# Attention results kept channels by tokens and normalised through DRAM, in a fused attention and GLU kernel

## The chip, the cores and the metric

One core of one Trainium2 chip. The metric is the device time of one launch, in microseconds. Before the change it is 891.36 us, the median of three runs (887.86, 891.71, 891.36).

## What is computed

One transformer block on 2048 tokens of 512 channels in float32, with 32 heads of 16 channels. The tokens are cut into four segments of 512. Within a segment there is causal softmax attention; across segments there is a running memory (M, z) that each segment reads before it adds to it:

```python
for s in range(N):
    p = softmax(qs @ ks.T * scale + mask)
    a_dot = p @ vs
    a_mem = (phi(qs) @ M) / (phi(qs) @ z + 1e-6)
    outs.append(g * a_mem + (1 - g) * a_dot)
    M, z = M + phi(ks).T @ vs, z + sum(phi(ks))
x = x + ga * (concat(outs) @ wo)
x = x + gb * ((h(x) @ w_gate) * (h(x) @ w_up)) @ w_down
```

Both halves begin with a layer norm that is scaled and shifted from c and w_mod.

## The kernel before

**Units and turns.** Attention is done in 32 units. Unit u is four heads of one segment (segment u//8, group of eight heads g = u//2 % 4, half u % 2). A main loop (from L998) runs turns v = -2 to 32, each of five slots. In turn v the scores of units v+1 and v+2 are formed once to find their row maxima (`q_step`: TensorE, then reductions on VectorE), the scores of unit v are formed again, transposed and with the maxima subtracted, and exponentiated (`k_step`: TensorE, then the 128x1024 `pt` on ScalarE, then the causal select on GpSimd), and in slot 1 the products with v of unit v-1 are summed (`av_step`: 32 matmuls `tb`, then the copy `tsb` on ScalarE). `tb` has 17 useful rows for each head, 16 channels and the sum of the exponentials.

The maxima (`nm`) are split into `nh`, transposed on TensorE (`ntp`), copied to `nt`, and two DMAs on the sync engine's queue (SP) put them into `qst`, where `k_step` of the next turn reads them (`n_split`, `n_step`). k and q of a head group go through DRAM as well (`kd`, `qd`), and `load` brings them back as `kst` and `qst`, three turns ahead.

**The result of a unit.** `t_step`, in slot 4 of turn v, transposes `tsb` of unit v-1 with four TensorE transposes into `tr` (tokens by channels), takes the reciprocal of the sums and multiplies, both on VectorE, into `orow`. After the second half of a head group GpSimd adds the memory term `memb`, which had been written to `memd` by `a_mem` and read back, and a DMA stores `orow` in `od`, tokens by channels. When the output projection comes, `wo_load` reads `od` back (`orl`), `wo_op` transposes it to channels by tokens with four transposes for each head group (`op`), and splits it into a high part `oH` (ScalarE) and a rest `oL` (VectorE). `wo_mm` multiplies both by wo (`wops`).

**Fill.** Everything else that TensorE has to do (projections `kps`, `qps`, `vps`, memory, output projection, second layer norm) comes from two generators, `fill_a` and `fill_b`, which give pieces of work into four of the five slots. Each piece costs credit, and a turn brings 5.5 of it, which is 24 matmuls of 512 columns; a piece that yields False ends its slot at once, and unused credit is kept for later turns. `fill_b` starts when `fill_a` is done: it opens new pools, loads wo and `orl`, and runs `wo_op` and `wo_mm` of segments 0, 1 and 2. Segment 3 comes after the loop, and then the GLU.

TensorE runs in the order of the program, and so does VectorE from the loop on. The order on ScalarE, GpSimd and SP is set by the scheduler, but each of them takes its instructions strictly in turn: what waits holds up what stands behind.

Below, "interval u" is the time from the copy `tsb` of unit u-1 to that of unit u.

Of the kernel before, what the change touches and what calls it, by code (L numbers as in the profile page):

```python
# [58 lines left out]
def tile_kernel(ctx, tc, x, wq, wk_, wv, wo, beta, w_gate, w_up, w_down, c, w_mod, out):  # L59
# [76 lines left out]
    od = [dram.tile([4, P, D], F32, name=f"od{s}") for s in range(NSEG)]  # L136
# [64 lines left out]
    def ln(pool, hpool, xt, s, sc, sh, pfx, hb, fast, kept_h=None):  # L201
# [5 lines left out]
        for d in range(KT):  # L207
            h = pool.tile([P, L], F32, tag="hf" if kept_h is None else "orl", name=f"{pfx}hf{s}_{d}", bufs=hb[2])
# [45 lines left out]
    orows, mems, ptiles, sels, tbs, tsbs = {}, {}, {}, {}, {}, {}  # L254
# [76 lines left out]
    def av_step(u, kb):  # L331
# [19 lines left out]
        if kb == 2:  # L351
            tsbs[u] = ap.tile([P, L], F32, tag="tsb", name=f"tsb{u}", bufs=2)
            act.activation(tsbs[u], tbs.pop(u), AF.Copy)  # L353

    def t_step(u):

        s, g, jq = u // 8, u // 2 % 4, u % 2
        ug = u // 2
        h0 = jq * HQ
        if jq == 0:  # L360
            orows[ug] = wpool.tile([P, 4, HG, DH], F32, tag="orow", name=f"orow{ug}", bufs=2)
            if s > 0:
                mems[ug] = ap.tile([P, 4, HG, DH], F32, tag="memb", name=f"memb{ug}", bufs=2)
                nc.sync.dma_start(mems[ug].rearrange("p t h e -> p (t h e)"), memd[s][g])
        orow = orows[ug]
        tsb = tsbs.pop(u)
        tr = pst([P, 4, 4, 32], "sm", f"tr{u}", F32)
# [6 lines left out]
        if jq == 0:  # L374
            return
        if s > 0:
            nc.gpsimd.tensor_add(orow, orow, mems.pop(ug))
        if ug < NSEG * NG - 1:
            nc.sync.dma_start(od[s].rearrange("t p c -> p t c")[:, :, g * P:(g + 1) * P],
                              orow.rearrange("p t h e -> p t (h e)"))  # L380
# [35 lines left out]
    def wo_load(s, pool):  # L416
        rw = []
        for t in range(4):
            a = pool.tile([P, D], F32, tag="orl", name=f"orl{s}_{t}", bufs=4)
            n = D - P if s == NSEG - 1 else D  # L420
            pin(nc.sync.dma_start(a[:, 0:n], od[s][t][:, 0:n]))
            rw.append(a)
        return rw

    def wo_op(s, pb, rw, us, gs=range(NG)):

        for g in gs:
            op = bank(f"op{s}_{g}")
            for t in range(4):
                a = rw[t][:, g * P:(g + 1) * P]  # L430
                if s == NSEG - 1 and g == NG - 1:
                    a = orows[NSEG * NG - 1][:, t].rearrange("p h e -> p (h e)")
                TP(op[:, t * P:(t + 1) * P], a, ident)
            oH = pb.tile([P, L], F32R, tag="oH", name=f"oH{s}_{g}", bufs=6)
            oL = pb.tile([P, L], F32R, tag="oL", name=f"oL{s}_{g}", bufs=6)
            act.activation(oH, op, AF.Copy)
            us.append((oH, oL))
            yield 0.45
            pin(vec.tensor_sub(oL, op, oH.bitcast(F32)))
            if g % 2 == 1:  # L440
                yield False
# [175 lines left out]
    stage = [("ph", 3), ("ph", 3), ("ph", 3), ("mem", 1), ("pkr", 1), ("f", 2)] + [("x", 4)] * 6  # L617
# [135 lines left out]
    memq, nkq = [], {}  # L753

    def mem_step():
        while memq:
            w = next(memq[0], None)
            if w is not None:
                return w
            memq.pop(0)  # L760
# [616 lines left out]
```

## Time and profile before

| | |
|---|---|
| median of three runs | 891.36 us |
| the profiled execution, its own time | 892.53 us |
| its span | 890.8 us |
| mean granted TensorE clock | 0.987 |
| TensorE matmuls busy | 848.3 us (95%) |
| VectorE busy | 660.8 us (74%) |
| ScalarE busy | 471.0 us (53%) |
| GpSimd busy | 417.9 us (47%) |
| moved by DMA | 124.85 MB, mean 140 GB/s |

The attention loop fills the span from about 60 us to 523 us, then comes a passage of some 60 us into the GLU, and the GLU runs to the end. In the rows of a timeline the first number is the start in us, the second the time until the last instruction of a merged row ended, and a bracket gives the idle time of the engine ahead of it and what ended it. Matmuls are pipelined, so what a matmul costs TensorE is read from the distance of two starts. "128x512 f32" is partitions by elements. In a row of windows the columns are the window's length, then busy time (and number of instructions) of TensorE, its weight loads, VectorE, ScalarE and GpSimd, then the granted clock, the busy share of the DMA engines, and GB/s.

### The profile page before, as it was taken

The numbers are of one execution on the slowest core, as the hardware profiler recorded it, in microseconds if no ns is written. First come the engines' busy times: TensorE is split into PE (matmuls) and PEld (weight loads), VectorE is DVE, ScalarE is ACT, GpSimd is POOL, SyncE is SP. The second block draws the span as 40 slices with busy tenths as digits, with TensorE's granted clock in tenths as the row PEclk, the third lists the DMA queues.
The fourth block names the chain that finished last, engine by engine and source line by source line (L and its number), as shares of the span: only waits on it lengthen the run. The fifth ranks groups of instructions, "written<-read, shape, count | busy, mean of one in ns | idle before, by whom it ended". The sixth has DMA issues, their size and how long they took to land.

```text
span 890.8 us, 14534 instructions
## 1 busy us (share of the span) xinstructions
PE 848.3 (95%) x4951; PEld 598.1 (67%) x4952; DVE 660.8 (74%) x1756; ACT 471.0 (53%) x730; POOL 417.9 (47%) x564
## 2 busy tenths in 40 slices
PE   8988999999999999999899898999999999999998
PEld 5755666665665556565556466878878888887886
DVE  8588877897788987678788649798884856666532
ACT  3756867777677775577444654333262622333321
POOL 4544545566546574466623423887500746560000
PEclk9998999999999999999899999999999999999999
DMA  7673543746446543657861453444402341222032
GB/s 237 216 229 114 185 122 104 240 155 199 139 125 201 163 140 123 184 164 225 257 214 61 131 164 105 144 143 123 167 26 97 93 140 48 71 54 92 0 116 95
DMA packets 103515, 124.85 MB, mean 140 GB/s; under 512 B 11984, under 2 KB 71376, under 8 KB 103440
## 3 DMA queue, kind: packets, MB, share of 16 engines
q1 hardware_dynamic: 103296, 123.90, 45.3%
q8 instruction: 39, 0.64, 0.3%
q14 instruction: 36, 0.29, 0.1%
q10 hardware_dynamic: 144, 0.02, 0.0%
HBM read 80.17 MB, written 43.45 MB: 139 GB/s over the span
## 4 chain that ended last, share of the span: by engine, by line
PE 65%; DVE 16%; DMA 8%; ACT 5%; POOL 3%; issue 2%; SPq 1%; DVEq 0%; POOLq 0%; ACTq 0%
PE g L86 20%; PE acc L86 14%; PE tb L86 6%; DVE q L40 6%; PE k L86 5%; PE q L86 5%; PE vps L86 4%; PE kps L86 2%; PE qps L86 2%; PE wops L86 2%; ACT pt L324 2%; DMA qd<-q 2%; DMA qst<-qd 1%; PE up L86 1%; DVE nm L40 1%
## 5 line engine op out<-in xcount | busy, mean ns | idle before, releaser
L40 DVE CUSTOM_DVE_ANT_0 q<-q,cmask 128x384 f32<-128x384 f32 (+3 forms) x512 | 246.7, 508 | 57.9 <-PE q L86 47.8
L324 ACT ACTIVATE pt<-k 128x1024 f32<-128x1024 f32 x160 | 163.8, 1024 | 76.5 <-PE k L86 74.2
L327 POOL TENSOR_SCALAR_AFFINE_SELECT pt<-pt 128x256 f32<-128x256 f32 (+1 forms) x224 | 99.0, 455 | 175.4 <-ACT pt L324 172.0
L86 PE MATMUL q<-kst,qst 96*128 96x384 bf16 (+3 forms) x512 | 102.4, 303 | 9.2 <-DVE nm L40 6.5
L86 PE MATMUL k<-qst,kst 98*128 98x384 bf16 (+3 forms) x512 | 98.4, 305 | 8.0 <-ACT pt L324 6.3
L400 POOL TENSOR_TENSOR w<-w 128x256 f32<-128x256 f32 (+1 forms) x84 | 72.4, 872 | 60.4 <-DMA w<-in_w_up_dram 57.8
L397 POOL TENSOR_TENSOR AL<-w,AH 128x512 fp32r<-128x512 f32 (+1 forms) x42 | 59.3, 1412 | 55.4 <-ACT AH L396 54.4
L86 PE MATMUL tb<-pt,v 128*32 128x512 f32 (+3 forms) x1024 | 76.3, 438 | 0.9 <-POOL pt L327 0.9
L86 PEld LDWEIGHTS <-kst 98*128 98x128 bf16 x512 | 39.0, 99 | 50.9 <-issue 42.8
L40 DVE DVE_READ_ACCUMULATOR2_ANT nm<- 128x1 f32 x512 | 72.0, 141 | 0.0
L396 ACT ACTIVATE AH<-w 128x512 fp32r<-128x512 f32 (+2 forms) x88 | 47.3, 565 | 45.7 <-POOL w L400 22.4
L86 PEld LDWEIGHTS <-qst 96*128 96x128 bf16 x512 | 43.8, 98 | 36.2 <-issue 10.0
L1319 DVE TENSOR_TENSOR mL<-mid,mH 128x512 fp32r<-128x512 f32 (+1 forms) x44 | 32.2, 735 | 41.5 <-ACT mH L1318 40.5
L86 PE MATMUL acc<-DH,mH 128*128 128x512 f32 x144 | 57.2, 397 | 0.0
L86 PE MATMUL acc<-DH,mL 128*128 128x512 f32 x144 | 56.6, 393 | 0.2 <-DVE mL L1319 0.2
L86 PE MATMUL acc<-DL,mH 128*128 128x512 f32 x144 | 56.5, 393 | 0.0
L86 PEld LDWEIGHTS tb<-pt,v 128*32 128x32 f32 x1024 | 28.7, 110 | 40.4 <-issue 34.7
L1318 ACT ACTIVATE mH<-mid 128x512 fp32r<-128x512 f32 (+1 forms) x44 | 27.1, 626 | 51.2 <-PE acc L86 50.2
L1114 ACT ACTIVATE p<-g 128x512 f32<-128x512 f32 (+1 forms) x22 | 13.1, 597 | 69.2 <-PE g L86 69.2
L397 DVE TENSOR_TENSOR AL<-w,AH 128x512 fp32r<-128x512 f32 (+3 forms) x44 | 33.8, 772 | 18.5 <-ACT AH L396 18.5
L353 ACT ACTIVATE tsb<-tb 128x512 f32<-128x512 f32 x32 | 19.1, 596 | 38.7 <-PE tb L86 38.6
L86 PE MATMUL g<-t_0H,AH 128*128 128x512 f32 (+1 forms) x88 | 34.6, 394 | 1.1 <-DVE u L1123 1.0
(278 smaller groups left out, 2097.9 us busy)
## 6 DMA issues: line engine op xcount, KB each, us to landing
kst<-kd SPq DMA_DIRECT2D x32, 384.0 KB, 4.3
qst<-qd SPq DMA_DIRECT2D x32, 384.0 KB, 5.1
wm<-in_w_mod_dram SPq DMA_DIRECT2D x24, 256.0 KB, 5.2
kd<-k SPq DMA_DIRECT2D x16, 384.0 KB, 3.8
qd<-q SPq DMA_DIRECT2D x16, 384.0 KB, 3.2
w<-in_w_gate_dram SPq DMA_DIRECT2D x40, 128.0 KB, 2.5
w<-in_w_up_dram SPq DMA_DIRECT2D x40, 128.0 KB, 3.1
wd<-dwd SPq DMA_DIRECT2D x6, 768.0 KB, 4.6
```

What stands on the lines that cost most here:

```text
L40: i = getattr(self.eng, name)(*a, **k)
L86: return pe(nc.tensor.matmul(*a, **k))
L324: lpt[0] = act.activation(pt, kp, AF.Exp, scale=0.25)
L327: sels[u, i] = nc.gpsimd.affine_select(w, w, pattern=[[0, w.shape[1]], [1, P]], compare_op=ALU.is_ge, fill=0.0, base=0, channel_multiplier=-1)
L353: act.activation(tsbs[u], tbs.pop(u), AF.Copy)
L396: pin(act.activation(hi[sl], w[sl], AF.Copy))
L397: eng.tensor_sub(lo[sl], w[sl], hi[sl].bitcast(F32))
L400: pin(ce.tensor_tensor(w[:, o, :, 0:n], w[:, x, :, 0:n], w[:, y, :, 0:n], op=op))
L1114: act.activation(r["p1"], ps, AF.Copy)
L1318: pin(act.activation(mH[0:n], md[0:n], AF.Copy))
L1319: vec.tensor_sub(mL[0:n], md[0:n], mH[0:n].bitcast(F32))
```

## The change

- `t_step` no longer transposes. `tsb` stays channels by tokens. Right after the copy, `av_step` stores it in DRAM (`td`) with a DMA on ScalarE's queue. In slot 4 `t_step` loads the sums (`rd`, 128 partitions of 16) and the channels (`orow`, now 128 x 512 channels by tokens).
- New steps `r_step` and `o_step` follow in the next two turns, each part in a slot of its own: the reciprocal of `rd` on VectorE, its DMA to `rdd`, a load that repeats it over the 16 channels of each head (`rb`), then on GpSimd `orow` times `rb` and plus `memb`, then the DMA to `od`.
- The memory term is transposed to the same layout by a step of its own (`a_memT`: four transposes `mT`, a copy `mTs` on ScalarE), after the rest of the memory work. `memb` is loaded later.
- `wo_op` reads `od` as it is, without transposes, and makes the rest in place. In `fill_b` its steps, woven with those that prepare wo, take one slot each (`paced`) and no credit, and `wo_mm` of segment 0 comes ahead of the wait for segment 2.
- The last head group keeps the old path, with transposes; the one before it skips `od`.
- Smaller: two buffers for `mem`, a buffer of its own for `hf`, and another spread of the GLU's weight preparation in its first steps.

```diff
         if kb == 2:
             tsbs[u] = ap.tile([P, L], F32, tag="tsb", name=f"tsb{u}", bufs=2)
             act.activation(tsbs[u], tbs.pop(u), AF.Copy)
+            if not last(u // 2):
+                nc.scalar.dma_start(td[u], tsbs.pop(u))
...
-        for t in range(4):
-            TP(tr[:, t].rearrange("p a b -> p (a b)"), tsb[:, t * P:(t + 1) * P], ident)
-        rd = ap.tile([P, 4, 4], F32, tag="rd", name=f"rd{u}", bufs=2)
-        vec.reciprocal(rd, tr[:, :, :, DH])
-        vec.tensor_mul(orow[:, :, h0:h0 + 4, :], tr[:, :, :, 0:DH],
-                             rd.unsqueeze(3).to_broadcast([P, 4, 4, DH]))
...
+        tv = td[u].rearrange("(j r) t -> j r t", r=32)
+        nc.sync.dma_start(rds[ug][:, jq], tv[:, DH].rearrange("j (p k) -> j p k", k=DH))
+        nc.sync.dma_start(orows[ug][h0 * DH:(h0 + HQ) * DH], tv[:, 0:DH])
+
+    def r_step(ug, i):
+
+        if i == 0:
+            vec.reciprocal(rds[ug], rds[ug])
+        elif i == 1:
+            nc.sync.dma_start(rdd[ug].rearrange("(q a) (p k) -> (a p) q k", a=HQ, k=DH), rds.pop(ug))
+        else:
+            rds[ug] = ap.tile([P, L], F32, tag="rb", name=f"rb{ug}", bufs=1)
+            nc.sync.dma_start(rds[ug], rdd[ug].unsqueeze(1).to_broadcast([HG, DH, L]))
+
+    def o_step(ug, i):
+
+        s, g = ug // NG, ug % NG
+        o = orows[ug]
+        if i == 0:
+            nc.gpsimd.tensor_mul(o, o, rds.pop(ug))
             if s > 0:
+                nc.gpsimd.tensor_add(o, o, mems.pop(ug))
...
+        if not direct(s, g):
+            nc.sync.dma_start(od[s][g], o)
...
-                TP(op[:, t * P:(t + 1) * P], a, ident)
...
+    def a_memT(s, g, mem):
+
+        mT = pst((P, L), "sm", f"mT{s}_{g}")
+        for t in range(4):
+            TP(mT[:, t * P:(t + 1) * P], mem[:, t].rearrange("p h e -> p (h e)"), ident)
+        mTs = pa.tile([P, L], F32, tag="mTs", name=f"mTs{s}_{g}", bufs=1)
+        act.activation(mTs, mT, AF.Copy)
+        nc.sync.dma_start(memd[s][g], mTs)
...
-        yield from weave(wo_op(0, pb, B["orl"], us[0]), ob, (0, 1, 2, 3))
+        yield from paced(both(wo_op(0, pb, B["orl"], us[0]), ob))
+        yield from weave(wo_mm(0, us[0], pb), both(pr, wo_op(1, pb, o1, us[1])), (1, 3, 4, 6, 7, 9, 10, 12, 13))
```

Three places in the order of instructions. First ScalarE, at the copy `tsb` of a unit of segment 1. Before:

```order
L353 ACTIVATE tsb_1377<-tb_1360 128x512
L324 ACTIVATE pt_1_1382<-k_1_1379 128x1024
L553 ACTIVATE wm_0_1193<-wm_0_1193,s_c 128x512
L324 ACTIVATE pt_2_1414<-k_2_1409 128x1024
L665 ACTIVATE v_0_166<-vps_0_1402 128x32x16
```

and after, at the same unit:

```order
L355 ACTIVATE tsb_1412<-tb_1395 128x512
L326 ACTIVATE pt_1_1419<-k_1_1416 128x1024
L357 DMA td_145<-tsb_1412 128x512
L605 ACTIVATE wm_0_1235<-wm_0_1235,s_c 128x512
L326 ACTIVATE pt_2_1452<-k_2_1447 128x1024
L717 ACTIVATE v_0_211<-vps_0_1440 128x32x16
```

The store of `td` stands behind the next exponential here; at other units it stands ahead of it, with the copy `pkr` or nothing between it and `tsb`.

Second TensorE, where `fill_b` begins (interval 25 before; the same slots of interval 27 after). Before, the transposes of `wo_op` stand between the scores of two units:

```order
L86 LDWEIGHTS qst_189
L86 MATMUL q_1_1_5418<-kst_185,qst_189 128x128
L89 MATMUL op_0_5451<-ident,orl_0_4704 128x128
L89 MATMUL op_0_5451<-ident,orl_1_4706 128x128
L89 MATMUL op_0_5451<-ident,orl_2_4708 128x128
L89 MATMUL op_0_5451<-ident,orl_3_4710 128x128
L86 LDWEIGHTS kst_183
L86 MATMUL k_3_5473<-qst_187,kst_183 128x384
```

After, nothing stands there:

```order
L86 LDWEIGHTS qst_232
L86 MATMUL q_1_1_5769<-kst_228,qst_232 128x128
L86 LDWEIGHTS kst_230
L86 MATMUL k_3_5775<-qst_234,kst_230 128x384
L86 LDWEIGHTS kst_230
L86 MATMUL k_3_5775<-qst_234,kst_230 128x128
```

All of interval 27 after is like that: TensorE has the scores, `ntp` and `tb`, and no fill. Interval 26 has two matmuls `up` and four transposes `mT` beside them. In interval 28 stand 69 matmuls `wops`, one behind the other, where before 24, 9 and 30 of them and 16 transposes `op` were spread over intervals 26 to 28.

Third SP, at the DMAs that follow one unit. Before:

```order
L304 DMA qst_187<-nt_1576 1x16x128 x2
L379 DMA od_139<-orow_1458 128x4x128
L259 DMA kst_182<-kd_0_111 96x2048
L259 DMA qst_186<-qd_0_95 96x2048
L499 DMA wm_3_1715<-in_w_mod_dram 128x512
```

After:

```order
L390 DMA rd_1497<-td_146 128x1x16
L306 DMA qst_232<-nt_1613 1x16x128 x2
L391 DMA orow_1496<-td_146 64x1x512
L261 DMA kst_227<-kd_0_111 96x2048
L261 DMA qst_231<-qd_0_95 96x2048
```

The load of the sums, which has to wait until the store of `td` has landed, stands ahead of the two DMAs that bring the maxima to `qst`. It does so for at least 17 of the 30 units that go this way.

More of the change, by code (lines that the diff above doesn't have):

```diff
@@ L1 @@
 from contextlib import ExitStack
-from itertools import chain
+from itertools import chain, islice
 import concourse.bass as bass
@@ L370, in t_step @@
[L370 to L380 removed]
+            orows[ug] = wpool.tile([P, L], F32, tag="orow", name=f"orow{ug}", bufs=2)
```

142 lines of the change are left out of this document (93 added, 49 removed).

## The prediction

> **What bounds the kernel now.** I read the busy times first, then the chain of waits, and then the windows of the attention loop.
>
> ```profile
> PE 848.3 (95%) x4951; PEld 598.1 (67%) x4952; DVE 660.8 (74%) x1756; ACT 471.0 (53%) x730; POOL 417.9 (47%) x564
> PE 65%; DVE 16%; DMA 8%; ACT 5%; POOL 3%; issue 2%; SPq 1%; DVEq 0%; POOLq 0%; ACTq 0%
> 719.46 106.96 PE g L86 x462
> ```
>
> The first line says that TensorE is busy for 95% of the span, the second that 65% of the chain that ended last runs through it, the third that at full clock one matmul of 512 columns costs 106.96 / 462 = 0.2315 us. The 16% of VectorE show that it is not TensorE everywhere. Where, the windows tell:
>
> ```profile
> 100.00:140.00 40.00, 40.00 (x281) 24.42 (x279) 31.04 (x114) 28.37 (x39) 17.35 (x29) 1.00 0.48 139
> 300.00:340.00 40.00, 36.51 (x284) 22.84 (x284) 32.39 (x118) 28.37 (x43) 26.19 (x37) 1.00 0.51 161
> 420.00:460.00 40.00, 35.95 (x232) 23.13 (x230) 30.76 (x103) 20.94 (x29) 20.21 (x30) 0.91 0.69 218
> 460.00:500.00 40.00, 35.97 (x250) 21.17 (x251) 32.10 (x112) 19.10 (x25) 11.85 (x24) 0.96 0.28 93
> ```
>
> Where fill is thick (first line) TensorE does not stop; later a tenth of it is idle. VectorE is busy for 31 to 32 of 40, ScalarE and GpSimd have more room. The length of a unit is read from the copies `tsb`:
>
> ```profile
> 122.03 0.60 ACT L353 ACTIVATE tsb<-tb 128x512 f32<-128x512 f32 x1 [1.09 <-PE tb L86]
> 135.24 0.60 ACT L353 ACTIVATE tsb<-tb 128x512 f32<-128x512 f32 x1 [1.68 <-PE tb L86]
> 416.98 0.59 ACT L353 ACTIVATE tsb<-tb 128x512 f32<-128x512 f32 x1
> 438.56 0.60 ACT L353 ACTIVATE tsb<-tb 128x512 f32<-128x512 f32 x1 [1.74 <-PE tb L86]
> 481.15 0.60 ACT L353 ACTIVATE tsb<-tb 128x512 f32<-128x512 f32 x1
> 522.82 0.60 ACT L353 ACTIVATE tsb<-tb 128x512 f32<-128x512 f32 x1 [2.61 <-PE tb L86]
> L353 ACT ACTIVATE tsb<-tb x32: 585/597/603, 76.2 to 522.8; 128x512 f32<-128x512 f32 x32
> ```
>
> The first two bound interval 4: 13.21 us, packed. Intervals 1 to 24 (76.2 to 416.98) take 14.2 on average. Interval 25, the first of `fill_b`, takes 21.58; intervals 25 to 28 together 64.2, and 29 to 31 41.7 us. In interval 25 TensorE stops, and its clock falls:
>
> ```profile
> 424.05 0.66 PE L89 MATMUL op<-ident,orl 128*128 128x128 f32 x4 [1.03 <-DVE oL L40]
> 426.35 0.66 PE L89 MATMUL op<-ident,orl 128*128 128x128 f32 x4 [1.64 <-DVE oL L40]
> 424.00:428.00 4.00, 2.31 (x16) 1.58 (x16) 3.14 (x8) 2.45 (x5) 3.78 (x3) 1.00 0.95 295
> 428.00:432.00 4.00, 3.21 (x9) 2.50 (x9) 3.93 (x11) 2.17 (x3) 1.92 (x3) 0.50 1.09 347
> 530.74 0.50 PE L86 MATMUL wops<-woH,oH 128*128 128x512 f32 x1 [1.98 <-DVE oL L40]
> ```
>
> Transposes `op` wait for the rest `oL` of an earlier group; in the window that has only 2.31 us of TensorE work of 4, the clock is still 1.00, and in the next 0.50. The last row is the same wait behind the loop.
>
> **What the change removes from TensorE.** 30 units lose four transposes `tr`, 15 head groups lose four `op`, and 11 head groups gain four `mT`.
>
> ```profile
> 127.66 0.60 PE L89 MATMUL tr<-ident,tsb 128*128 128x128 f32 x4
> 128.02 0.48 PE L86 MATMUL vps<-wvH,ahH 128*128 128x512 f32 x1
> ```
>
> From start to start four transposes cost 0.36 us. So 30 x 0.36 = 10.8 and 15 x 0.36 = 5.4 go and 11 x 0.36 = 4.0 come: 12.2 us of TensorE. An interval keeps it only where TensorE sets the length, so I add up by stage, against the profiled 892.53 us.
>
> *Intervals 1 to 24.* 24 groups `tr` go (8.6) and 10 `mT` come (3.6): 5.0 net. The windows show it packed at one place and 91% at another; I take three quarters, **-3.8** (bounds 0 and -5.0).
>
> *Intervals 25 to 28.* A unit without fill has 13.21 - 24 x 0.2315 - 0.36 = 7.3 us of TensorE work (interval 4's, less its fill and its transposes). After, by the order: interval 25 has 21 matmuls of fill, where interval 4 had 24, and I give it the same 13.2 (floor 7.3 + 21 x 0.2315 = 12.2). Interval 26 has two and four transposes, 27 nothing: there VectorE decides.
>
> ```profile
> L40 DVE CUSTOM_DVE_ANT_0 q<-q,cmask 128x384 f32<-128x384 f32 (+3 forms) x512 | 246.7, 508 | 57.9 <-PE q L86 47.8
> L40 DVE DVE_READ_ACCUMULATOR2_ANT nm<- 128x1 f32 x512 | 72.0, 141 | 0.0
> L324 ACT ACTIVATE pt<-k 128x1024 f32<-128x1024 f32 x160 | 163.8, 1024 | 76.5 <-PE k L86 74.2
> ```
>
> The reductions are (246.7 + 72.0) / 32 = 10.0 us a unit, a floor; a packed interval, 13.2, is the ceiling, and I take 11.5 between. ScalarE's `pt` are 5.1, and interval 26 adds eight copies `oH` and four of wo at some 0.6, so it stays under that. Interval 28 has 69 `wops`: 69 x 0.2315 + 7.3 = 23.3. Together 13.2 + 11.5 + 11.5 + 23.3 = 59.5 against 64.2: **-4.7** (55.5 to 62.9 by the bounds, -8.7 to -1.3). The stall of interval 25 goes, but most of it comes back as intervals that TensorE does not fill.
>
> *Intervals 29 to 31.* 24 `wops`, 18 with 16 small transposes, 24: each about 13, 39 against 41.7: **-2.5** (0 to -3).
>
> *Behind the loop.* Three groups `op` go (1.1), and of the wait at 530.74 I count a half, since `oH` and `oL` of the last group keep their chain: **-2.0** (0 to -3).
>
> Sum: 892.53 - 13.0 = 879.5, **880 us**. The profiled execution is 1.2 above the median, and the three runs are 3.9 apart, so I do not correct for that.
>
> **What I cost at nothing, and its cover.**
>
> ```profile
> L40 DVE TENSOR_TENSOR orow<-tr,rd x32: 423/424/427, 87.6 to 530.9; 128x256 f32<-128x256 f32 x32
> L40 DVE RECIPROCAL rd<-tr x32: 244/251/256, 87.3 to 530.6; 128x16 f32<-128x16 f32 x32
> 419.73 0.35 DVE L40 RECIPROCAL den<-den 128x32 f32<-128x32 f32 x1
> L377 POOL TENSOR_TENSOR orow<-orow,memb x12: 1262/1275/1662, 215.4 to 531.4; 128x512 f32<-128x512 f32 x12
> L779 ACT ACTIVATE pkr<-mp x12: 581/597/600, 50.5 to 322.1; 128x512 f32<-128x512 f32 x12
> L533 ACTq DMA_DIRECT2D be<-in_beta_dram x1: 386/386/386, 0.8 to 0.8; - x1
> q1 hardware_dynamic: 103296, 123.90, 45.3%
> ```
>
> VectorE loses 30 x 0.675 = 20.3 us and gains 15 reciprocals of 0.35 = 5.3. GpSimd gains 15 products of 1.275 = 19 us; it is busy for 17 to 26 of 40. A select `pt` queued behind a product is late by up to 1.3 us, and `av_step` takes it a turn later. ScalarE gains 11 copies `mTs` (6.6 us) and 30 issues; the one issue of its queue took 0.386, so 11.6 us, before or behind the next exponential. If that is not covered, the bound is 18 us over 446, the second rival below. The queues carry 30 stores and loads of units and 15 each of sums more, some 16 MB on 124 at a share of 45%, and SP some 90 issues of about 0.4 = 36 us over 446. None of these engines is full. What is not sure is what stands in front of what.
>
> **The added wait.** On SP the load of `rd` waits for the landing of `td`, and behind it stand the two DMAs that bring the maxima to `qst`.
>
> ```profile
> L379 SPq DMA_DIRECT2D od<-orow x15: 371/382/667, 103.2 to 506.9; - x15
> DMA to landing us min/median/max: 2.4/3.9/6.7
> 125.22 1.15 SPq L304 DMA_DIRECT2D qst<-nt  x2
> 131.84 0.61 PE L86 MATMUL k<-qst,kst 98*128 98x512 bf16 x2
> DMA to landing us min/median/max: 1.6/1.7/6.6
> ```
>
> The nearest row to `td` is the store `od` of the same size: 2.4 to 6.7 us to landing, 3.9 in the middle. In interval 4 `tsb` would end at 122.63, `td` be issued behind the `pt` at about 123.6 + 0.4, and land at 127.9 rather than the 125.2 at which the maxima go now. They take 1.15 us of issue and 1.7 to land (the last row), after 0.4 for `rd`: 131.2, while the scores start at 131.84. So the median is covered, by 0.6 us. A landing of 6.7 makes it 134.0, 2.1 late. I take the median, at no cost; the upper end is the last rival. That is the thinnest cover in the sum.
>
> [...]
>
> **The rivals.**
>
> *All of it is kept: 870.* If the intervals with fill stay packed and those without are short, the 12.2 us of TensorE, the 8.4 by which interval 25 exceeds interval 4 and 2 behind the loop go: 892.5 - 22.6. For: the packed first window. Against: 69 `wops` in one interval, while two intervals stand with TensorE at 7.3 of at least 10.
>
> *Nothing is kept: 891.* If the chain through scores, exponential and select sets the intervals, ScalarE's 18 us of new work meet it and eat the 13.0 but for 1 or 2. For: from 300 to 340 TensorE stands a tenth although there is fill. Against: ScalarE is busy for 28 of 40 at most.
>
> *Half clock in intervals 26 and 27: 887.* 7.3 us of TensorE at half clock are 14.6, 3.1 over the 11.5, twice, and then some 3 us of interval 28 until the clock is back, half of them lost: 879.5 + 6.2 + 1.5 = 887.2. For: the rows of 424 to 432. Against: with 7.3 of 11.5 TensorE is busier than it was there.
>
> *Slower, SP's queue holds the maxima: 902.* Place: the load of `rd` ahead of `nt`, in at least 17 units. Price: at a landing of 5.8 us, between the middle and the longest of `od`, the scores start 1.3 late by the working above, and 17 x 1.3 = 22 us on 880. It decides from a landing of 3.9 + 0.6 = 4.5 us where the store goes behind a `pt`, and of about one `pt`, 1.0, more where it goes ahead. For: half of the stores `od` took longer than 3.9. Against: another store of 256 KB took less:
>
> ```profile
> memd<-mem SPq DMA_DIRECT2D x12, 256.0 KB, 2.8
> ```
>
>
> That the transposes do not go is excluded by the order; that what replaces them is as dear is the second rival.
>
> **How the numbers follow.** Forecast 0.50, all kept 0.15, nothing kept 0.15, half clock 0.08, held maxima 0.12. The forecast's own bounds by the stages are 0 to -5.0, -8.7 to -1.3, 0 to -3 and 0 to -3; taken together they rarely lie at one end, and give 874 to 887. The range takes in the rivals at 870 and 891 with some 2 to 3 us on either side and leaves out the slower one: 868 to 894. About 0.5%, 4.5 us, is what a measurement of this kernel can tell from no change, so faster means below 886.9 and slower above 895.8. Faster: 0.50 + 0.15 and three eighths of the half clock, 0.68. Within: 0.15 and the rest of the half clock, 0.20. Slower: 0.12.
>
> **What the profile after would show.** If the sum holds, TensorE's busy time falls by about 12 us; intervals 1 to 24 take about 14.0; no interval has a gap in front of `op`; intervals 26 and 27 take 11.5 each with a clock of 1.00, and 28 about 23. Held maxima would show as TensorE's `k` waiting for the DMAs of `nt`, which now is 1.7 us in all, and as a longer distance from `ntp` to `qst`. The second rival would show as longer waits of GpSimd for `pt`, and intervals 1 to 24 at 14.2 or more. The forecast is wrong above all if stores of `td` land later than 4.5 us in most units, or if VectorE, which now stands in for TensorE in intervals 26 and 27, takes well over 11.5.

## The result and the profile after

The changed kernel takes 926.11 us, the median of four runs (924.71 to 932.0), against 889.61 for the kernel before in the same comparison: a ratio of 1.0423, with a 95% interval of 1.0367 to 1.0478. That is 4% slower, and 46 us from the 880 of the forecast, above its range. The profiled execution is the slowest of the four (932.0 us; the mean clock of the other three is 0.966 to 0.968), so its stages add up to some 6 us more than the median. From its page the busy times and the chain of waits, and its mean clock:

```profile
PE 856.8 (92%) x4815; PEld 596.3 (64%) x4816; DVE 647.8 (70%) x1711; ACT 476.6 (51%) x741; POOL 436.0 (47%) x579
PE 63%; DMA 11%; DVE 10%; POOL 6%; ACT 5%; issue 4%; SPq 1%; ACTq 0%; POOLq 0%; DVEq 0%
core 0: 930.2 us, clock 0.957
```

TensorE has 136 matmuls fewer than before and is busy for 8.5 us more. At half clock a matmul takes nearly twice as long (in the kernel before, `wops` start 0.43 us apart from 429.42 to 431.98 us, at a clock of 0.50, against 0.2315 at full clock), and the mean clock fell from 0.987 to 0.957. The chain shows who took over: DMA from 8% to 11%, GpSimd from 3% to 6%, and VectorE fell from 16% to 10%. Where the time lies is read from the copies `tsb`, now at L355. The first, that of unit 4, that of unit 24 and the last:

```profile
79.16 0.60 ACT L355 ACTIVATE tsb<-tb 128x512 f32<-128x512 f32 x1 [2.02 <-PE tb L86]
136.85 0.60 ACT L355 ACTIVATE tsb<-tb 128x512 f32<-128x512 f32 x1 [1.68 <-PE tb L86]
440.01 0.60 ACT L355 ACTIVATE tsb<-tb 128x512 f32<-128x512 f32 x1 [1.73 <-PE tb L86]
564.37 0.60 ACT L355 ACTIVATE tsb<-tb 128x512 f32<-128x512 f32 x1 [0.38 <-PE tb L86]
```

| us of the profiled execution | before | sum of the prediction | after |
|---|---|---|---|
| up to the first copy | 76.2 | 76.2 | 79.2 |
| intervals 1 to 24 | 340.7 | 336.9 | 360.9 |
| intervals 25 to 31 | 105.8 | 98.5 | 124.4 |
| behind the last copy | 368.0 | 366.0 | 365.8 |
| span | 890.8 | 877.6 | 930.2 |

(The second column is the first less 3.8, 7.2 and 2.0; the time is 1.7 above the span.)

Two passages lost, 20.1 and 18.5 us, and the end gained its 2.2. Up to the first copy, profiled executions of the kernels below lie between 74 and 79 us, whatever their edit, so those 2.9 say nothing. Single intervals differ by 1 to 3 us between the profiled executions of these kernels as well, intervals 16 and 28 by 6 to 7 (14.2 to 20.1 and 24.5 to 31.5 in the kernels with P and without U); only sums and repeated differences are relied on below.

Intervals 1 to 4 have one product on GpSimd (at 118.23, in interval 3) and take 57.7 us, against 59.0 before. Interval 4 and interval 16 of the changed kernel, in the columns of a row of windows:

```profile
124.09:136.85 12.76, 12.76 (x90) 7.79 (x89) 9.01 (x36) 6.65 (x9) 3.83 (x8) 1.00 0.55 172
298.89:321.06 22.17, 15.46 (x102) 10.09 (x103) 12.91 (x47) 10.40 (x18) 7.51 (x15) 0.85 0.58 176
```

In the first TensorE is packed and the interval is 0.45 shorter than before (13.21): four transposes less, as reckoned. In the second, TensorE lacks 6.7 of 22.17 us, and the clock is 0.85. The waits that are new or have grown (who waits, for whom; us, times, the longest):

```profile
POOL orow L408 <- DMA rb<-rdd: 36.7, 10, 6.0
PE k L86 <- ACT pt L326: 23.4, 21, 5.6
ACT oH L478 <- DMA orl<-od: 12.1, 4, 6.1
PE q L86 <- DMA qst<-qd: 9.2, 3, 6.0
ACT mTs L875 <- DMA memd<-mTs: 4.2, 2, 2.7
PE k L86 <- DMA qst<-nt: 3.6, 3, 2.0
```

The first line is the one that the forecast did not have: the product of `orow` and `rb` on GpSimd waits for the load of `rb`. With waits that the profile puts down to other causes, GpSimd stands for 55.7 us in all ahead of the 15 products. What such a wait costs is seen in interval 7, which takes 18.3 us (14.5 before). One row each of GpSimd, ScalarE and TensorE of the changed kernel:

```profile
173.33 1.29 POOL L408 TENSOR_TENSOR orow<-orow,rb 128x512 f32<-128x512 f32 x1 [5.98 <-DMA rb<-rdd]
176.49 0.62 ACT L763 CAST k<-kr 128x512 bf16<-128x512 f32 x1 [4.75 <-POOL kr L755]
178.09 1.01 PE L86 MATMUL k<-qst,kst 98*128 98x512 bf16 x2 [3.40 <-ACT pt L326]
```

GpSimd waits for `rb` and makes `kr` behind the product; on ScalarE the recast of `k` waits for `kr`, and the next exponential `pt` stands behind it; TensorE waits for that `pt`. A second way, ahead of interval 16: first SP, then GpSimd, then TensorE of the changed kernel:

```profile
286.50 0.65 SPq L401 DMA_DIRECT2D rb<-rdd  x1
...
296.42 0.38 SPq L770 DMA_DIRECT2D qd<-q  x1
...
300.96 0.79 SPq L261 DMA_DIRECT2D qst<-qd  x2
```

```profile
290.24 1.28 POOL L408 TENSOR_TENSOR orow<-orow,rb 128x512 f32<-128x512 f32 x1 [2.37 <-issue]
291.48 0.77 POOL L329 TENSOR_SCALAR_AFFINE_SELECT pt<-pt 128x256 f32<-128x256 f32 x2
292.21 1.28 POOL L410 TENSOR_TENSOR orow<-orow,memb 128x512 f32<-128x512 f32 x1
293.45 1.16 POOL L764 TENSOR_TENSOR q<-qr,q 128x512 bf16<-128x512 f32 x1
```

```profile
305.88 1.03 PE L86 MATMUL q<-kst,qst 96*128 96x512 bf16 x2 [6.04 <-DMA qst<-qd]
```

GpSimd stands for 2.37 us in front of the product (the profile names no releaser here, only "issue"; that it is `rb` is inferred from its load at 286.50). Behind it come selects `pt`, the memory term and the recast of `q`; that one ends at 294.6, goes out to `qd` at 296.42, comes back to `qst` from 300.96 on, and TensorE, which needs it for the scores, stands 6.04 us. A wait on GpSimd can reach TensorE through two DMAs as well. But only some 2.4 us of these 6.04 are the product's: with P below TensorE waits 3.67 at this place, without any product 3.48, and interval 16 still takes 19.1 and 21.2 us.

### The profile page after: what moved, and what is told of

Read it like the earlier page. It is cut to its first block, busy times and chain, and to the rows that moved or that the text cites. A ratio compares the mean times of both kernels' runs of the same rounds, so it can differ in the third digit from the quotient of the medians.

```text
span 930.2 us, 14431 instructions
## 1 busy us (share of the span) xinstructions
PE 856.8 (92%) x4815; PEld 596.3 (64%) x4816; DVE 647.8 (70%) x1711; ACT 476.6 (51%) x741; POOL 436.0 (47%) x579
## 2 busy tenths in 40 slices
DMA packets 113763, 140.54 MB, mean 151 GB/s; under 512 B 20696, under 2 KB 71896, under 8 KB 113688
## 4 chain that ended last, share of the span: by engine, by line
PE 63%; DMA 11%; DVE 10%; POOL 6%; ACT 5%; issue 4%; SPq 1%; ACTq 0%; POOLq 0%; DVEq 0%
PE g L86 22%; PE acc L86 13%; PE k L86 5%; PE q L86 5%; PE tb L86 5%; DVE q L40 4%; PE vps L86 3%; PE kps L86 3%; DMA qd<-q 2%; PE wops L86 2%; ACT pt L326 2%; DMA qst<-qd 2%; POOL pt L329 2%; PE qps L86 1%; DMA rdd<-rd 1%
## 5 line engine op out<-in xcount | busy, mean ns | idle before, releaser
L86 PE MATMUL k<-qst,kst 98*128 98x384 bf16 (+3 forms) x512 | 102.8, 316 | 27.4 <-ACT pt L326 23.4
L86 PE MATMUL q<-kst,qst 96*128 96x384 bf16 (+3 forms) x512 | 107.9, 317 | 21.7 <-DVE nm L40 12.2
L86 PEld LDWEIGHTS <-kst 98*128 98x128 bf16 x512 | 41.6, 102 | 75.4 <-issue 63.4
L86 PE MATMUL tb<-pt,v 128*32 128x512 f32 (+3 forms) x1024 | 84.4, 467 | 5.5 <-POOL pt L329 5.4
L435 ACT ACTIVATE AH<-w 128x512 fp32r<-128x512 f32 (+2 forms) x88 | 46.8, 564 | 40.6 <-POOL w L439 18.5
L1189 ACT ACTIVATE p<-g 128x512 f32<-128x512 f32 (+1 forms) x22 | 13.2, 599 | 75.9 <-PE g L86 75.9
L436 DVE TENSOR_TENSOR AL<-w,AH 128x512 fp32r<-128x512 f32 (+3 forms) x44 | 38.5, 876 | 15.7 <-ACT AH L435 15.5
L408 POOL TENSOR_TENSOR orow<-orow,rb 128x512 f32<-128x512 f32 x15 | 19.2, 1281 | 55.7 <-DMA rb<-rdd 36.7
L355 ACT ACTIVATE tsb<-tb 128x512 f32<-128x512 f32 x32 | 19.1, 596 | 41.8 <-PE tb L86 41.8
```

The costliest lines, as they stand in the source:

```text
L86: return pe(nc.tensor.matmul(*a, **k))
L408: nc.gpsimd.tensor_mul(o, o, rds.pop(ug))
L435: pin(act.activation(hi[sl], w[sl], AF.Copy))
L436: eng.tensor_sub(lo[sl], w[sl], hi[sl].bitcast(F32))
L1189: act.activation(r["p1"], ps, AF.Copy)
```

## The experiments

Each kernel is the changed one with the edits that are named, except where the kernel before is. P is the product's place on GpSimd, S the place of `rd` on SP, M the buffers of `mTs`, O the place of `oH` on ScalarE, U the output projection's steps as before. A ratio is to runs of the kernel before on the same chip, with its 95% interval. The groups of kernels ran on different chips (the four from P to "P, O" on one, the four behind them on a second, the last three on a third), so across groups the ratios count more than the medians. The stages, in us, are intervals 5 to 24 and 25 to 31 of one profiled execution.

| edit | median us | ratio | 5 to 24 | 25 to 31 |
|---|---|---|---|---|
| kernel before | 889.6 | 1 | 281.7 | 105.8 |
| changed kernel | 926.1 | 1.0423 (1.0367 to 1.0478) | 303.2 | 124.4 |
| P | 906.5 | 1.0202 (1.0163 to 1.0242) | 290.2 | 115.6 |
| no division | 905.6 | 1.0166 (1.0117 to 1.0215) | 292.6 | 115.4 |
| O | 925.8 | 1.0421 (1.0378 to 1.0463) | 303.1 | 121.5 |
| P, O | 906.6 | 1.0195 (1.0146 to 1.0245) | 289.3 | 116.8 |
| P, M | 901.6 | 1.0112 (1.0077 to 1.0147) | 284.9 | 116.2 |
| P, U | 906.6 | 1.0162 (1.0125 to 1.0199) | 291.4 | 118.2 |
| P, `td` on SP | 919.0 | 1.0311 (1.0284 to 1.0338) | 294.3 | 123.0 |
| P, S | 901.7 | 1.0115 (1.0089 to 1.0140) | 285.9 | 112.7 |
| P, M, S, O | 900.2 | 1.0094 (1.0059 to 1.0128) | 284.8 | 112.1 |
| P, M, S, O, U | 897.0 | 1.0066 (1.0038 to 1.0094) | 287.0 | 111.5 |
| P, M, S, O, first line of U | 901.6 | 1.0109 (1.0055 to 1.0163) | 283.7 | 112.8 |

**P: the product later on GpSimd.** `pin` orders an instruction behind the last TensorE instruction ahead of it in the program; without it the scheduler is free to put it earlier.

```diff
-            nc.gpsimd.tensor_mul(o, o, rds.pop(ug))
+            pin(nc.gpsimd.tensor_mul(o, o, rds.pop(ug)))
```

> The changed kernel, with the product of orow and rb ordered behind the TensorE instruction ahead of which it stands in the program, so that it stands one or two selects later in GpSimd's order. TensorE's order is the same. Theory P (GpSimd: the product waits for rb, 36.7 us in 10 times, and the selects and the recasts of k and q wait behind it): the idle time ahead of the product falls from 55.7 to under 20 us, intervals 1 to 24 fall from 360.7 to about 345 us, and the time from 926 to about 910. Theory S (SP's queue: the loads of rd and rb and the store of rdd hold up the maxima and the k and q transfers there): nothing of that changes, intervals 1 to 24 stay at 358 to 362 and the time at 924 to 928. Theory V (16 MB more through DMA): as S.

906.53 us: 20 us less, as theory P had it. The product stands a few instructions later (in interval 7 behind `kr` and the selects that had stood behind it), and its wait is gone:

```profile
POOL orow L408 <- DMA rb<-rdd: 1.4, 2, 0.9
```

TensorE's order is the same, and so are the bytes. The place of 15 instructions on GpSimd is worth more than half of the loss. Interval 7 takes 13.9 to 14.4 us in every version of the changed kernel below with P or without the product on GpSimd; in the two that keep the product in its old place, the changed kernel and O, it takes 18.3 and 19.9. In the profiled executions intervals 5 to 24 fell by 13.0 us and 25 to 31, where products stand as well, by 8.8.

**The changed kernel without the division.**

```diff
-            vec.reciprocal(rds[ug], rds[ug])
...
-            nc.sync.dma_start(rds[ug], rdd[ug].unsqueeze(1).to_broadcast([HG, DH, L]))
+            rds.pop(ug)
...
-            nc.gpsimd.tensor_mul(o, o, rds.pop(ug))
```

> The changed kernel without the division by the sums for the 15 head groups that go through td: no reciprocal, no rdd, no rb, no product (this part of the computation is left out). The stores td and the loads of rd and orow stay, so does the wait of SP for the landing of td. Theory P: intervals 1 to 24 fall from 360.7 to 340 or less, and the time to about 905. Theory S, in so far as it is the load of rd that waits: intervals 1 to 24 stay above 352, the time above 917. Theory V (volume): 4 MB of the 16 go, intervals 1 to 24 stay above 355.

905.62 us, the same as P by the intervals of both. So the reciprocal, the two DMAs and the product, once they wait for nothing, cost nothing that this shows; their wait cost 20. But intervals 5 to 24 do not come back to 281.7, so there is a rest that P does not explain.

**O: the copies `oH` later on ScalarE; and both.**

```diff
-            act.activation(oH, a, AF.Copy)
+            pin(act.activation(oH, a, AF.Copy))
```

> The changed kernel, with each copy oH of wo_op ordered behind the TensorE instruction ahead of which it stands in the program; the order on ScalarE alone changes, from interval 26 on. Theory A (ScalarE: eight oH stand in a row in interval 26 and four in 28, wait 12.1 us for loads of orl, and the exponentials wait behind them): the wait of oH for orl falls to under 4 us, intervals 25 to 31 fall from 124.5 to about 110 us, the time from 926 to about 911. Theory L (the work itself lies badly: two intervals without fill and then 69 wops in one, with the half clock that follows): intervals 25 to 31 stay above 119, the time above 920.

> Both edits of order at once, GpSimd's product and ScalarE's oH. P and A together: intervals 1 to 24 at about 345, 25 to 31 at about 110, time about 896. S and L: no gain, 920 to 928. If the two causes do not touch each other, the gain is the sum of the gains of the two alone within 3 us.

925.82 and 906.64: O is worth nothing that can be measured, alone or on top of P. The wait itself shrank, but did not go. In the first of these kernels it is

```profile
ACT oH L478 <- DMA orl<-od: 4.7, 1, 4.7
```

and in the second the longest of these waits still stands in interval 28, with an exponential and TensorE behind it:

```profile
482.74 0.63 ACT L478 ACTIVATE oH<-orl 128x512 fp32r<-128x512 f32 x1 [5.75 <-DMA orl<-od]
484.33 1.01 PE L86 MATMUL k<-qst,kst 98*128 98x384 bf16 x4 [4.02 <-ACT pt L326]
```

So the 15 us of theory A are not there, but O is no test of this one wait: its share of interval 28 stays open. In the same kernel the waits show another cause, on ScalarE at about 412 us:

```profile
412.69 0.60 ACT L875 ACTIVATE mTs<-mT 128x512 f32<-128x512 f32 x1 [3.56 <-DMA memd<-mTs]
413.18 1.02 ACT L326 ACTIVATE pt<-k 128x1024 f32<-128x1024 f32 x1
```

`mTs` has one buffer; the copy waits until the DMA of the one before has read it, and the exponential stands behind.

**M, U, the queue of `td`, and S, each on top of P.** For M the tile `rl4` shares the buffers of `rd`, to make room.

```diff
-        mTs = pa.tile([P, L], F32, tag="mTs", name=f"mTs{s}_{g}", bufs=1)
+        mTs = pa.tile([P, L], F32, tag="mTs", name=f"mTs{s}_{g}", bufs=2)
```

> The kernel with the product ordered later (906.5 us), and two buffers for mTs instead of one. Theory M (ScalarE: the copy mTs waits until the DMA of the copy before it has left its only buffer, 3.9 us in 3 times there and 6.4 with the copies oH ordered later too, and the exponentials stand behind it): that wait goes to 0, intervals 11 and 23, 16.9 and 18.0 us, fall to 14 to 15, and the time by 4 to 7 us to about 901. Rival: the intervals wait for something that is late anyway, and the time stays within 2 us of 906.

901.6 us, 5 less (8 by the ratios): M holds. Interval 11 fell from 16.9 to 13.4; it takes 13.4 in all seven kernels with M, and 16.9 to 17.0 in the four with P and neither M nor S. Interval 23 fell from 18.0 to 16.8, which says nothing: it takes 15.3 to 16.0 in four other kernels with P and without M.

```diff
-        yield from paced(both(wo_op(0, pb, B["orl"], us[0]), ob))
-        yield from weave(wo_mm(0, us[0], pb), both(pr, wo_op(1, pb, o1, us[1])), (1, 3, 4, 6, 7, 9, 10, 12, 13))
+        yield from both(wo_op(0, pb, B["orl"], us[0]), ob)
+        yield from weave(wo_mm(0, us[0], pb), pr, (3, 6, 9, 12))
+        yield from wo_op(1, pb, o1, us[1])
...
-        lr = islice(lg, 10)
-        yield from weave(wo_mm(1, us[1], pb), both(lr, wo_op(2, pb, o2, us[2])), (1, 5, 6, 7, 8, 9, 11, 12, 13, 14))
+        yield from weave(wo_mm(1, us[1], pb), lg, (1, 5, 6, 7, 8, 9, 11, 12, 13, 14))
         B["nxt"] = yield from lg
+        yield from wo_op(2, pb, o2, us[2])
```

> The kernel with the product ordered later (906.5 us), and the output projection's steps as the kernel before had them: the steps of wo_op no longer end their slots, wo_op of segments 1 and 2 comes after the matmuls of the segment ahead instead of between them. Theory L (two intervals without fill, then 69 wops in one, waits and half clock around them): the fill is spread, intervals 25 to 31 fall from 115.6 to about 106, the time to about 897. Theory A' (oH waits for loads of orl wherever it stands, and the exponentials with it): the wait of oH for orl stays at 8 us or more, and intervals 25 to 31 stay above 112, the time above 903.

906.6 us, no change of the median (3.6 us less by the ratios, whose intervals overlap), and intervals 25 to 31 at 118.2 instead of 106: L falls, and A' stands, with a wait of `oH` for `orl` of 14.2 us. Interval 28 fell from 26.3 to 18.3, but interval 26 rose from 19.2 to 31.5; the 69 matmuls that had lain in one interval now wait in another.

```diff
-                nc.scalar.dma_start(td[u], tsbs.pop(u))
+                nc.sync.dma_start(td[u], tsbs.pop(u))
```

> The kernel with the product ordered later (906.5 us), with the store td issued from SP's queue instead of ScalarE's; TensorE's and VectorE's orders are the same. Theory Q (30 issues on ScalarE's queue stand ahead of exponentials and cost it some 10 us, with waits in it): the time falls by 4 us or more, below 903. Rival R (SP's queue is where things are late; a store there has to wait for tsb and holds up what is behind it): the waits of TensorE for nt and for qst rise above the 12.1 and 10.8 us that they have now, and the time rises by 4 us or more, above 910. If neither queue matters: 904 to 909.

919.0 us, 12.5 more (9.7 by the ratios): of the two queues ScalarE's is the cheaper one for `td`. R holds for the maxima and not for the other half of what it named: the waits of TensorE for `qst` from `qd` fell, from 10.8 to 6.0 us. Those for the maxima about doubled, from 4.0 and 8.1 to

```profile
PE k L86 <- DMA qst<-nt: 9.1, 6, 3.2
PEld L86 <- DMA qst<-nt: 13.9, 8, 3.7
```

S turns this around: the loads of `rd` and `orow` go behind `nt` on SP.

```diff
-        nc.sync.dma_start(rds[ug][:, jq], tv[:, DH].rearrange("j (p k) -> j p k", k=DH))
-        nc.sync.dma_start(orows[ug][h0 * DH:(h0 + HQ) * DH], tv[:, 0:DH])
+        pin(nc.sync.dma_start(rds[ug][:, jq], tv[:, DH].rearrange("j (p k) -> j p k", k=DH)))
+        pin(nc.sync.dma_start(orows[ug][h0 * DH:(h0 + HQ) * DH], tv[:, 0:DH]))
```

> The kernel with the product ordered later (906.5 us), with the loads of rd and orow ordered behind the TensorE instruction ahead of which they stand in the program; on SP's queue the load of rd then stands behind the two DMAs of nt in all units, where it stood ahead of them in more than half; TensorE's order is the same. Theory S (my rival of before: the load of rd, which waits for the landing of td, holds up the maxima): the waits of TensorE for nt (4.0 us, and 8.1 on its weight loads) fall to the 1.7 and 2.1 of the kernel before, intervals 5 to 24 fall from 290.2 to about 285, the time to about 900. Rival: the loads come late anyway, and what is won for nt is lost on rd, rb and the product: 904 to 909.

901.67 us, 5 less (7.7 by the ratios): the gain that S forecast. What the edit took away is SP's own wait for the landing of `td`. With P, and then with P and S:

```profile
SPq L390 <- DMA td<-tsb: 45.7, 14, 5.7
SPq L390 <- DMA td<-tsb: 3.4, 3, 1.8
```

That the gain came by way of the maxima is not shown. TensorE's waits for them fell to 3.3 and 5.3, not to the 1.7 and 2.1 of the kernel before, and they differ as much between kernels without S (1.7 and 3.0 with P and O, 5.1 and 7.8 with P and M) and with it (5.9 and 6.5, 1.8 and 1.8 in the next two).

**All together.** First P, M, S and O; then U with them; then only the first line of U, so that no slot is ended and the weaving stays.

> The changed kernel with four edits together: the product later on GpSimd, two buffers for mTs, the loads of rd and orow behind nt on SP, the copies oH later on ScalarE. If the causes P, M and S are separate, their gains add: 926 - 20 - 5 - 5 = 896, less 0 to 3 for oH, and intervals 5 to 24 fall to 281 or less (281.7 in the kernel before). If they shared one slack, the gains overlap: 899 to 902, intervals 5 to 24 at 284 or more. Intervals 25 to 31 stay at 110 to 113, since nothing here spreads the fill.

> The four edits, and the output projection's steps in the order of the kernel before: no slot is ended, wo_op of segments 1 and 2 behind the matmuls of the segment ahead. By TensorE's order the 69 wops that stood in interval 28 are then spread as 21, 24 and 24 over intervals 26 to 28. Theory L: intervals 25 to 31 fall by what two unfilled intervals cost, from 112 to about 105, the time to about 888. Theory A' (interval 26 is as long as the chain of wo, woH, oH and their rests takes, whatever lies beside it, and the wops now wait for it in TensorE's order): intervals 25 to 31 stay at 110 or more, the time at 893 or more.

> As the last, but wo_op of segments 1 and 2 stays woven into the matmuls of the segment ahead, as in the changed kernel; only the ended slots are gone. TensorE's fill is the same 21, 24, 24. If the place of the copies oH beside the exponentials matters by itself, this differs from the last by 3 us or more, to the slower side; if only the fill counts, the two agree within 2 us.

900.2, 897.0 and 901.6 us. M and S do not add: each alone brought 5 us, both with O 6.3 (8, 8 and 10 by the ratios), so for the greater part they gain the same time. The ratios of the three agree within their intervals. The last two differ by 4.7 us in the median, more than the 3 that were to show the place of `oH`, but the five runs of the last spread from 896.0 to 904.8, so this is unclear. The time stays far from L's 888: L falls again. All three stay slower than the kernel before. Interval 26 looks as A' has it. TensorE of the second of them, and the windows there:

```profile
437.84 0.50 PE L86 MATMUL wops<-woH,oH 128*128 128x512 f32 x1 [1.45 <-ACT woH L910]
...
444.80 0.80 PE L86 MATMUL wops<-woH,oH 128*128 128x512 f32 x1 [2.62 <-ACT woH L910]
447.73 0.80 PE L86 MATMUL wops<-woH,orl 128*128 128x512 f32 x1 [2.14 <-DVE orl L40]
```

```profile
434.00:438.00 4.00, 1.65 (x12) 0.79 (x10) 3.68 (x16) 3.80 (x7) 3.41 (x6) 1.00 0.92 310
438.00:442.00 4.00, 2.60 (x6) 1.08 (x6) 2.90 (x5) 1.87 (x4) 1.14 (x1) 0.77 0.50 172
442.00:446.00 4.00, 0.97 (x2) 0.29 (x1) 0.00 (x0) 1.26 (x2) 3.18 (x3) 0.50 0.99 346
446.00:450.00 4.00, 2.27 (x7) 1.19 (x8) 2.28 (x3) 0.76 (x2) 1.54 (x3) 0.50 1.09 363
450.00:454.00 4.00, 4.00 (x13) 2.73 (x12) 2.09 (x5) 0.89 (x1) 2.34 (x4) 0.52 0.31 110
```

`wops` wait for the parts of wo and of the results, and the clock is at half for some 14 us (0.50 through 442 to 450, and partly so in the windows of 0.77 and 0.52).

**What holds interval 26.** The next two leave out the two late loads of wo, in the kernel with P, M, S, O and U and, as the control, in the kernel before:

```diff
-        raws = B["raw"] + [wo_raw(k, pb, "x1", 4) for k in (2, 3)]
+        raws = B["raw"] + B["raw"]
```

> The four edits with the output projection in the order of the kernel before (897.0 us, interval 26 of 26.9), without the two loads of wo rows 256 to 511: the raw rows 0 to 255 are used twice (this part of the computation is replaced). Theory W (interval 26 is long because these loads are issued late on SP and the matmuls wops wait for them through GpSimd and ScalarE: 4.2 us of ScalarE, then half clock): interval 26 falls to 21 or less, the time to about 891. Rival: the chain of copies oH, their rests and the rests of wo decides; interval 26 stays at 25 or more, the time at 895 or more.

> The kernel before, without the same two loads of wo (rows 0 to 255 used twice; this part of the computation is replaced). By W the kernel before loses little to them, since GpSimd waited only 0.22 us for them there: interval 25 stays within 2 us of 21.6, the time within 2 us of before. If they cost as much there as after, interval 25 falls to 16 or less, the time to about 885.

894.5 us (1.0062, 1.0035 to 1.0089) and 891.2 (1.0013, 0.9993 to 1.0033). Interval 26 took 24.9, where W had 21 or less, and in the control interval 25 took 20.4: W falls as the sole cause. (The ratio hardly differs from the 1.0066 of the kernel with the loads, so the total does not show the 2.0 us.) Without the loads the first copy `oH` waits for something else, on ScalarE:

```profile
433.08 0.63 ACT L478 ACTIVATE oH<-orl 128x512 fp32r<-128x512 f32 x1 [4.21 <-DMA memd<-mem]
```

It reuses the memory of the last `mem`, whose store must have left it. So that was taken away too (no store, no memory term of the last head group):

```diff
-            if last(s * NG + g):
-                nc.sync.dma_start(memd[s][g], mem.rearrange("p t h e -> p (t h e)"))
...
-            if jq == 1:
-                nc.gpsimd.tensor_add(orows[ug], orows[ug], mems.pop(ug))
```

> The kernel without the loads of wo rows 256 to 511 (894.5 us, interval 26 of 24.9), and without the memory term of the last head group: its mem is not stored, not read back and not added (this part of the computation is left out as well). The first copy oH takes the place in memory that mem had, and waited 4.2 us for its store. Theory D (the two waits stand beside each other, so that taking away one shows the other): interval 26 now falls to 20 or less, and the time by 4 us or more, to 890 or less. Rival: the chain of copies and rests itself takes the time; interval 26 stays at 23 or more and the time at 893 or more.

892.9 us (1.0048, 1.0016 to 1.0080), interval 26 at 21.7: between the two expectations. Behind the one wait stood the other, and removing both brings 5 us of the interval; the store alone was not taken away, and the total is not set apart from the 894.5 by the intervals. What is left goes with the clock, in the windows of this last kernel, though how much of it the clock makes was not separated:

```profile
434.00:438.00 4.00, 2.60 (x4) 1.08 (x4) 3.97 (x7) 3.77 (x8) 3.45 (x3) 0.50 0.77 238
438.00:442.00 4.00, 3.35 (x10) 2.09 (x11) 2.40 (x4) 0.04 (x1) 0.04 (x1) 0.50 1.05 310
```

**The product on VectorE** (with P, M, S, O, U):

```diff
-            pin(nc.gpsimd.tensor_mul(o, o, rds.pop(ug)))
+            vec.tensor_mul(o, o, rds.pop(ug))
```

> The four edits with the output projection in the order of the kernel before (897.0 us), with the product of orow and rb on VectorE, in program order, instead of GpSimd; TensorE's order is the same. Theory G (GpSimd's 19 us of products still make its recasts of k and q late, and the loads of kst and qst with them: intervals 15, 16 and 18 at 16.0, 18.7 and 18.2): these fall by 1 to 2 us each, intervals 5 to 24 from 287.0 to about 282, the time to about 892. Rival: the product waits for rb on VectorE too, and the reductions behind it wait: no gain or a loss, 896 to 902.

894.7 us, a ratio of 1.0059 (1.0039 to 1.0078) against 1.0066 on GpSimd: no difference is shown. Of G's three intervals only 16 fell (18.7 to 16.4, within what it varies by); 15 and 18 stayed at 16.0 and 18.1, and they take 14.5 and 17.4 in the kernel without any product, against 13.3 and 15.2 before. So for 15 and 18 G falls, for 16 it stays open. No version was faster than the kernel before.

## Why the prediction was wrong, point by point

- **TensorE as the bound, and 0.36 us for four transposes: right.** Undisturbed intervals became shorter by about that (interval 4 by 0.45), and the passage behind the loop gained 2.2 where the sum had 2.0.
- **"What I cost at nothing, and its cover": the step that failed.** The product was costed at its own 1.275 us on an engine with room, and a select behind it at "late by up to 1.3 us". What counted was what the product waits for. `rb` is the end of a chain (store `td`, load `rd`, reciprocal, store `rdd`, load `rb`), the scheduler put the product ahead of its landing, and what stood behind it on GpSimd waited with it (in interval 7 `kr`, for which ScalarE stood 4.75 us). Its 36.7 us of waiting (55.7 us of standing ahead of the products in all) cost 20 us, by P. The prediction asked what a wait for a landing holds up, but only of SP. The 13.0 us of the sum did not appear either: with P, M, S, O and U intervals 1 to 4 gain 2.8, and the end had gained its 2.2 without them, but the rest of the loop is longer than before.
- **The slower rival, SP's queue holding the maxima: the place was right, the price was not, and the way is not shown.** From the issue of `td` to that of `rd`, which waits for its landing, the rows of the 30 units give 2.0 to 9.4 us, 3.5 in the middle: about the 3.9 taken from `od`; 7 of the 30 are over the 4.5 that were to decide. SP waited 41.7 us for these landings, but TensorE waited only 3.6 us for the maxima (and its weight loads 5.2), and S brought 5 to 8 us, not 22. The forecast had one slower mechanism; there were four: P, S, M and what holds interval 26.
- **M was not seen.** `mTs` was counted as 11 copies of 0.6 us on ScalarE. Its single buffer makes the copy wait for a DMA, and the exponentials with it: 5 us (8 by the ratios), shared with S.
- **Intervals 25 to 28 at 59.5: wrong, 78.0.** The 13.2 for interval 25 and 23.3 for the 69 `wops` were near the mark only without further stalls (interval 25 took 14.5; 28 took 31.3, and 24.5 with P and S). The 11.5 for an unfilled interval took VectorE's reductions as the limit. Interval 26 took 19.2: VectorE makes the rests of wo and of the results ahead of the reductions there (0.70 us at 463.63 and 1.35 at 464.67, each behind a wait for its copy), so TensorE's longest wait in it is for a maximum, at 467.00. Interval 27, with two such rests, took 13.1, at a mean clock of 0.61 (second row). "The stall of interval 25 goes" held for interval 25, but the rests, whose wait made that stall, now stand ahead of the reductions of 26.

```profile
467.00 0.59 PE L86 MATMUL q<-kst,qst 96*128 96x256 bf16 x2 [3.05 <-DVE nm L40]
473.69:486.77 13.08, 11.18 (x62) 4.63 (x62) 10.35 (x38) 6.11 (x9) 7.22 (x13) 0.61 0.50 130
```

- **Half clock as a rival of 0.08: too low.** In interval 27 it came: 13.1 us at a mean clock of 0.61 lie between the 11.5 of the sum and the rival's 14.6. Thin windows stand ahead of it, in the rows below. Up to 600 us the clock stands at 0.50 in four stretches in the kernel before and in fourteen in this one, and two of these begin with waits shown above (from 178.1 us, with the 3.40 for `pt`, and from 304.4, within the 6.04 for `qst`). The 3 us until the clock is back were the author's estimate: the stretches of the kernel before last 3.4 us twice (18.4 to 21.8 and 492.9 to 496.3) and 6.8 twice (83.3 to 90.1 and 428.0 to 434.8), and in this one the clock is back at 485.3, ahead of interval 28, and at 0.50 again from 505.8 to 512.6. The mean clock of 0.957 against 0.987 is some 28 us of full-speed time not granted (0.030 x 930). It lies within the stages above, not on top of them.

```profile
462.00:466.00 4.00, 1.21 (x7) 0.42 (x5) 2.37 (x5) 3.94 (x7) 2.12 (x3) 0.85 0.49 138
466.00:470.00 4.00, 2.67 (x12) 0.76 (x15) 3.86 (x19) 1.11 (x2) 0.75 (x1) 0.50 1.00 324
...
502.00:506.00 4.00, 0.14 (x1) 0.07 (x1) 0.41 (x3) 0.63 (x1) 0.00 (x0) 0.97 0.96 337
506.00:510.00 4.00, 2.24 (x8) 1.44 (x8) 0.76 (x3) 3.25 (x5) 0.86 (x3) 0.50 0.97 334
```

These are the changed kernel's intervals 26 and 28: each of these thin windows is followed by one at half clock, as in the rows of before. Not every thin window is, as the last section shows.

Settled are P (20 us), M and S (5 each alone, some 6 together, with O; by the ratios 8 and 10) and the choice of queue (12.5, or 9.7). Open is the rest of some 5 us (ratios of 1.005 to 1.007): with all five edits intervals 1 to 4 keep their gain of 2.8, but 5 to 24 take 5.3 more than before and 25 to 31 5.7 more. In the latter the chain that prepares wo and the results, with the half clock behind it, holds interval 26; in the former intervals 8, 15, 16 and 18 are each 2.5 to 3.2 us longer than before, with single waits of TensorE of 1.5 us for maxima (15), 2.0 for `qst` from `qd` (16) and 1.6 for `x` (18), whose cause was not isolated. That the changed kernel moves 15.7 MB more (140.54 against 124.85) was not tested by itself; without the division it moves 136.35, and was no faster than with P.

## What to carry to other kernels

Before work of the bounding engine is replaced by a trip through DRAM, see that each instruction that waits for a landing stands, on its own engine, behind everything that is due sooner: look at the engine's order for every consumer in the chain, and price what stands behind it, not its duration. Where a scheduler sets that order, one instruction tied to its place in the program can be worth more than the change itself (here 20 us by P, where the change was to bring 13.0). A single buffer that a DMA empties is such a wait too (5 us by M), and where two waits stand side by side, removing one shows the other (interval 26 took 24.9 us without the late loads of wo, 21.7 without the store and the memory term of the last head group as well).

## What the runs showed of the hardware that was not expected

A stall of TensorE can cost more than itself: behind some thin windows the clock went to 0.50 and stayed there. In the changed kernel TensorE stood for 5.62 us up to 507.76 and was busy for 0.14 us of the 4 from 502 to 506; the clock was at 0.50 from 505.8 to 512.6. In the kernel before it was busy for 2.31 of the 4 from 424 to 428, with no gap over 1.64; the clock was at 0.50 from 428.0 to 434.8. In the kernel without the last memory term it was busy for 2.02 of the 4 from 430 to 434; the clock was at 0.50 for the next 8 us and at 0.73 in the 4 behind them. Up to 600 us the stretches at 0.50 last 3.4 to 6.8 us in the kernel before and 3.4 to 10.3 in the changed one. It does not always: in the kernel with P

```profile
484.00:488.00 4.00, 1.05 (x6) 0.57 (x5) 1.15 (x6) 2.39 (x4) 0.15 (x1) 1.00 0.99 354
488.00:492.00 4.00, 4.00 (x25) 3.00 (x24) 2.96 (x10) 2.77 (x4) 1.56 (x5) 1.00 0.42 139
```

the clock stays at 1.00, so the busy share of 4 us alone does not decide, and what does is not shown here. From 434 to 442 in the kernel without the last memory term TensorE was busy for 2.60 and 3.35 of each 4 us, at 0.50 throughout; the clock came back in the window behind them, in which TensorE was busy for 4.00:

```profile
442.00:446.00 4.00, 4.00 (x19) 2.84 (x17) 2.47 (x6) 2.09 (x3) 3.27 (x5) 0.73 0.67 240
```
